# Moving the softmax bias to ScalarE, keeping a sum in PSUM, and rescheduling the end of attention and the output-weight splits

## The chip, the cores and the metric

The kernel runs on one core of a Trainium2 chip. A core has a matrix engine (TensorE, PE in the profile), a vector engine (VectorE, DVE), a scalar engine (ScalarE, ACT), a general-purpose engine (GpSimd, POOL) and an engine that mostly issues DMA transfers (SyncE, SP). Each engine works through its own queue in order and waits on semaphores for the others. The metric is the device time of one execution in microseconds (us), as a median over runs.

## The reference

Two independent computations on inputs with 2048 rows and 1024 columns, whose results stand side by side in the output.

```python
# A: attention with 32 heads of width 32 and a sliding window of 256 keys
q, k, v = split(x @ wqkv)                       # 2048 x 1024 each
scores = (q @ k.T) * 32 ** -0.5                 # per head
scores = where(0 <= i - j < 256, scores, -1e9)
o = softmax(scores) @ v
a = o @ wo
# B: Fourier mixing, real part, by matrix products
ar, ai = xb @ hid_re.T, xb @ hid_im.T
b = seq_re @ ar - seq_im @ ai
out = concat([a, b])
```

All inputs are float32. The kernel splits every float32 operand into a high and a low float16 half (`split`: ScalarE writes the high half, VectorE the difference) and makes each product of three float16 passes.

## The kernel before

The work runs in this order on TensorE. First 96 products for q, k and v, then 64 "units" of Fourier mixing, numbered 0 to 63 in names such as `u61`, `un61_a`, `p2_61_0`, then 8 output products `po`. A unit is of kind x (two products of 24 matmuls) or c (seven products of 12 matmuls, made by `seven`, in which three accumulating PSUM banks `m0`, `m1`, `m2` are drained after each product by ScalarE or VectorE into the `y` tiles). Units 56 to 63 are the last eight of kind c; the code calls their place among the eight `i`, so that `i == 5` is unit 61, `i == 6` unit 62 and `i == 7` unit 63. While a unit runs, the next unit's operands are loaded (`raw_u`), scanned for their largest value on ScalarE (`junk`), reduced through a transposition on TensorE (`pt_u`, `sc_u`) and split (`un62_a`, `un62_b`, `un62_c`); four differences of a unit are made on GpSimd (L621, `gsub`).

Attention runs underneath from product 24 on. It has 256 blocks (128 queries, two heads). `tick` is called every 4 or 8 matmuls and advances the attention generator at a constant `rate`, so that attention ends about 0.7 units before `i == LAST`; there a loop emits what is left, the attention pool `att` is closed and the pool `late` takes its place in SBUF. A block goes through the engines like this:

- TensorE writes scores to one of two PSUM buffers `s` (L210).
- VectorE masks (L218), takes the negative row maximum `mx` (L220) and makes the bias of the exponential, `bias = mx * es + PSHIFT` (L223), two numbers a partition.
- ScalarE takes the exponential, one head at a time, with that bias (L230), and the high half (L233); VectorE makes the low half (L234), which frees the scores' buffer.
- SP transposes both halves by a DMA (L236); GpSimd masks the transposed tile (L248, L250) behind a small instruction `mark` that reads `bias` (L227).
- For each second block TensorE multiplies by v into the only buffer of the pool `ps_v` (tag `pv`, L277). VectorE takes the reciprocal of the row sums (L283), adds the two halves of o into the SBUF tile `os` (L285) and multiplies them by the reciprocal (L288). The transposition `pt_u` of a unit's scale uses the same PSUM buffer.

After attention the output weight `wo` is loaded in eight pieces of 512 KB (`raw_wo0_0` to `raw_wo3_1`), and made into seven operands in two halves: 14 "fills" (a `split` each, into `reg2` and `ext`) and 8 differences on GpSimd. `o_load` and `o_blocks` fetch attention's result and combine it into the operands of the output products (L804, L753, L806, L813).

The order of instructions on each engine is set by a scheduler when the program is built, from the order of the code, the buffers and estimated durations; `tc.issue_after` pins an instruction behind another one.

Of the kernel before, what the change touches and what calls it, by code (L numbers as in the profile page):

```python
# [9 lines left out]
F32 = mybir.dt.float32  # L10
# [40 lines left out]
def fused_kernel(ctx: ExitStack, tc: tile.TileContext, xa, wqk, wv, wo, xb, wd, cs, out):  # L51
# [35 lines left out]

    nbank = [0]
# [50 lines left out]
    def scale_of(key, v, s, down=2.0 ** -14):  # L139

        pt = ps_v.tile([P, 2, 2, VW], F32, tag="pv", name=f"pt_{key}")
        pt = pt.rearrange("p r h w -> p (r h w)")[:, :P]
# [27 lines left out]
    def attention():  # L170
# [22 lines left out]
        def s_step(b, j):  # L193
# [29 lines left out]
            nc.vector.tensor_scalar(bias, mx, es, PSHIFT, op0=ALU.mult, op1=ALU.add)  # L223
# [30 lines left out]
        def v_step(b):  # L254

            g, sc, hp, i = blocks[b]
            pvt = ps_v.tile([P, 2, 2, VW], F32, tag="pv", name=f"pv_{b}")
# [26 lines left out]
            os_ = att.tile([P, 2, 2, DH], F32, tag="os", name=f"os_{b}")  # L284
# [77 lines left out]
    LAST = 6  # L362
# [396 lines left out]
    def wo_blocks(late, i):  # L759

        b1, b2, b3, b4 = (load_raw(wo[b % 2, 2 * (b // 2) + i], [2, CH], f"wo{b}_{i}", late) for b in range(4))

        def fill(pos, raw):
            o = slot(pos)
            split(o[:, 0, 2 * i:2 * i + 2], o[:, 1, 2 * i:2 * i + 2], raw, vwo[:, 1:2])

        def step(turn):
            if turn == 0:
                fill(0, b1)
                gsub(b2, b2, b1)  # L770
            elif turn == 1:
                fill(6, b4)
                gsub(b4, b4, b2)
            elif turn == 2:
                fill(3, b3)
                gsub(b1, b4, b1)
            elif turn == 3:
                fill(4, b2)
                gsub(b3, b3, b4)
            elif turn == 4:  # L780
                fill(2, b4)
            elif turn == 5:
                fill(1, b1)
            elif turn == 6:
                fill(5, b3)

        return step
# [56 lines left out]
    with tc.tile_pool(name="pb", bufs=1) as pb:  # L844
# [62 lines left out]
        for n, (kind, p, c, i) in enumerate(units):  # L907
# [21 lines left out]
            if p == 1 and c == 1:  # L929
                if i == LAST:  # L930
# [7 lines left out]
                    wo_step = wo_blocks(late, 0)  # L938
                if i == LAST + 1:
                    wo_step = wo_blocks(late, 1)  # L940
            late_unit = p == 1 and c == 1 and i >= LAST

            def turned(turn):
                hook(n, turn)
                if late_unit:
                    wo_step(turn)

# [17 lines left out]
            seven(f"p2_{n}", i, uns.pop(n), lambda pos: tsum[:, TPOS[pos]], done, turned)  # L965
            if p == 1 and c == 1 and i == 6:
                o_load(0)
                o_load(1)
                o_blocks(late, 0)
# [63 lines left out]
```

## Time and profile before

| | |
|---|---|
| median of 3 runs | 1881.85 us (1872.96, 1881.85, 1882.64) |
| profiled execution | 1872.75 us |
| its span (first to last instruction) | 1870.9 us |
| TensorE busy | 1776.4 us (95%) |
| VectorE busy | 1349.3 us (72%) |
| ScalarE busy | 984.0 us (53%) |
| GpSimd busy | 670.2 us (36%) |

A row of the groups reads: line, engine, operation, output<-input, shapes, count | busy us, mean ns of one | idle time of the engine ahead of it, and what ended that. In the table of windows the columns are the stretch, its length, busy us and instructions of PE, PEld (weight loads), DVE, ACT and POOL, the mean clock that TensorE was granted (1.00 is full), the share of time the DMA engines were busy and GB/s. The stage names that the prediction uses are: 645 to 1640 us, units with attention underneath; 1640 to 1712 us, the end of the units, where the output weight is prepared; 1712 us to the end, the output products.

### The profile page before, as it was taken

The page shows a single profiled execution, that of the slowest core. Times are in us where ns is not written, and L with a number is a line of the kernel's source. Part 1 is how long each engine was busy: PE and PEld are TensorE (multiplying, and loading weights), DVE is VectorE, ACT ScalarE, POOL GpSimd, SP SyncE. Part 2 cuts the span into 40 slices and gives each one's busy share as a digit, 9 for nine tenths or more (in the row PEclk, how much of TensorE's full clock was granted, in tenths as well). Part 3 has the DMA queues.
Part 4 walks back from the last instruction along what each step waited for, and adds up shares of the span by engine and source line. Part 5 has one row for each costly group of instructions (what it writes and reads, how often), then busy time and mean ns, then how long its engine had stood idle before and what let it go on. Part 6 is the DMA issues. An engine that isn't in the chain of part 4 may idle for free.

```text
span 1870.9 us, 30051 instructions
## 1 busy us (share of the span) xinstructions
PE 1776.4 (95%) x10876; PEld 860.7 (46%) x10876; DVE 1349.3 (72%) x2470; ACT 984.0 (53%) x1567; POOL 670.2 (36%) x849
## 2 busy tenths in 40 slices
PE   7999999999999999999989999988999999879998
PEld 3444555445555544544444444543444445424443
DVE  7665788777666688876787876786787688686551
ACT  3233444454445567755566665675575676543221
POOL 0000122122213554543454543544555456654000
PEclk9999999999999999999999999999999999989999
DMA  5457899886676557777359889557899549865341
GB/s 225 127 180 198 219 240 233 229 217 153 164 166 139 107 127 181 194 184 173 74 123 193 174 178 207 108 125 141 165 175 213 105 105 147 135 163 96 99 120 68
DMA packets 440596, 297.95 MB, mean 159 GB/s; under 512 B 339072, under 2 KB 396416, under 8 KB 440448
## 3 DMA queue, kind: packets, MB, share of 16 engines
q1 hardware_dynamic: 433536, 270.87, 59.9%
q0 software_dynamic: 6912, 25.17, 8.3%
q8 instruction: 85, 1.39, 0.3%
q14 instruction: 63, 0.52, 0.1%
HBM read 146.93 MB, written 75.63 MB: 119 GB/s over the span
## 4 chain that ended last, share of the span: by engine, by line
PE 64%; DVE 12%; DMA 8%; issue 5%; ACT 5%; POOL 5%; SPq 0%; POOLq 0%; ACTq 0%; DVEq 0%
PE p L834 14%; PE p L342 12%; PE pk L342 9%; PE pv L342 8%; PE po L834 8%; PE pq L342 7%; DMA t<-hl 4%; PE s L210 3%; PE pv L277 3%; POOL raw_u L621 2%; DVE reg L104 1%; ACT s L230 1%; DVE mx L220 1%; DMA raw_wd<-in_wd_dram 1%; POOL t L250 1%
## 5 line engine op out<-in xcount | busy, mean ns | idle before, releaser
L230 ACT ACTIVATE s<-s,bias,escs 128x256 f32<-128x256 f32 (+1 forms) x512 | 267.2, 530 | 330.1 <-DVE bias L223 280.6
L342 PE MATMUL p<-reg,un 128*128 128x512 f16 x1536 | 351.4, 383 | 1.9 <-DVE un L104 1.9
L234 DVE TENSOR_TENSOR hl<-s,hl 128x512 f16<-128x512 f32 (+1 forms) x256 | 169.7, 667 | 88.0 <-ACT hl L233 87.4
L342 PEld LDWEIGHTS <-un 128*128 128x128 f16 x1536 | 147.5, 98 | 170.9 <-issue 6.6
L227 POOL TENSOR_SCALAR mark<-bias 128x1 f32<-128x1 f32 x128 | 38.9, 304 | 509.3 <-DVE bias L223 465.2
L834 PE MATMUL p<-reg,un_b 128*128 128x512 f16 x768 | 189.7, 392 | 18.0 <-ACT reg L956 5.7
L834 PE MATMUL p<-reg,un_a 128*128 128x512 f16 x768 | 187.9, 386 | 9.9 <-DVE y L954 7.4
L342 PE MATMUL pq<-reg,wu_q 128*128 128x512 f16 x768 | 177.9, 386 | 7.4 <-ACT reg L109 4.3
L834 PE MATMUL p<-reg,un_c 128*128 128x512 f16 x768 | 180.5, 382 | 3.5 <-ACT y L956 1.9
L342 PE MATMUL pk<-reg,wu_k 128*128 128x512 f16 x768 | 174.7, 381 | 2.3 <-ACT wu_k L109 1.6
L621 POOL TENSOR_TENSOR raw_u<-raw_u,raw_u 128x512 f32<-128x512 f32 x96 | 138.8, 1446 | 95.4 <-DVE un_a L104 91.4
L342 PE MATMUL pv<-reg,reg 128*128 128x512 f16 x768 | 172.7, 379 | 0.0
L220 DVE TENSOR_REDUCE mx<-s 128x2 f32<-128x512 f32 (+1 forms) x256 | 170.1, 668 | 2.8
L248 POOL TENSOR_SCALAR_AFFINE_SELECT z<-t 128x512 f16<-128x512 f16 x224 | 156.2, 718 | 36.4 <-DMA t<-hl 29.8
L250 POOL TENSOR_SCALAR_AFFINE_SELECT t<-t 128x512 f16<-128x512 f16 x224 | 166.2, 765 | 0.1
L233 ACT ACTIVATE hl<-s 128x512 f16<-128x512 f32 (+1 forms) x256 | 147.7, 585 | 9.6 <-DMA t<-hl 5.4
L218 DVE COPY_PREDICATED s<-upper,s 128x256 f32<-128x256 uint32 x224 | 93.7, 422 | 70.8 <-PE s L210 68.6
L210 PE MATMUL s<-qk,qk 96*128 96x128 f16 (+2 forms) x704 | 127.5, 277 | 13.9 <-DVE hl L234 13.7
L834 PEld LDWEIGHTS <-un_b 128*128 128x128 f16 x768 | 74.3, 100 | 105.8 <-issue 26.6
L277 PE MATMUL pv<-vt,t 128*128 128x65 f16 x1984 | 114.9, 186 | 7.7 <-POOL t L250 7.6
L342 PEld LDWEIGHTS <-wu_q 128*128 128x128 f16 x768 | 75.0, 99 | 96.3 <-issue 13.1
L834 PEld LDWEIGHTS <-un_a 128*128 128x128 f16 x768 | 74.2, 99 | 95.9 <-issue 12.9
(166 smaller groups left out, 2827.5 us busy)
## 6 DMA issues: line engine op xcount, KB each, us to landing
raw_u<-in_cs_dram SPq DMA_DIRECT2D x64, 512.0 KB, 4.9
qk<-qs SPq DMA_DIRECT2D x192, 128.0 KB, 3.4
out_dram<-y POOLq DMA_DIRECT2D x36, 512.0 KB, 7.4
raw_u<-in_xb_dram SPq DMA_DIRECT2D x32, 512.0 KB, 5.2
vs<-yv SPq DMA_DIRECT2D x32, 260.0 KB, 2.6
vt<-vs SPq DMA_DIRECT2D x32, 260.0 KB, 3.5
raw_x<-in_xa_dram SPq DMA_DIRECT2D x16, 512.0 KB, 10.2
qs<-yq SPq DMA_DIRECT2D x32, 256.0 KB, 2.5
```

The costliest lines, as they stand in the source:

```text
L210: nc.tensor.matmul(s[:, j, at:at + (k1 - k0) * P], q2s[g, sc][:, h, i * P:i * P + P], k2s[g, k0 // QB][:, h, k0 % QB * P:k0 % QB * P + (k1 ...
L218: nc.vector.copy_predicated(s[:, :, 2 * P:3 * P], upper2, s[:, :, :P] if nb == 3 else never2)
L220: nc.vector.tensor_reduce(mx, sv, axis=AX.X, op=ALU.max, negate=True)
L230: nc.scalar.activation(sv[:, h], sv[:, h], AF.Exp, bias=bias[:, h:h + 1], scale=es)
L233: nc.scalar.activation(hi, sv, AF.Copy)
L234: behind[:] = [nc.vector.tensor_tensor(lo, sv, hi, op=ALU.subtract)]
L248: nc.gpsimd.affine_select(out=z, in_=pk, compare_op=ALU.is_gt, fill=0.0, base=0, pattern=[[0, 4], [-1, P]], channel_multiplier=1)
L250: nc.gpsimd.affine_select(out=pk, in_=pk, compare_op=ALU.is_ge, fill=0.0, base=0, pattern=[[0, 4], [1, P]], channel_multiplier=-1)
L277: nc.tensor.matmul(pvt[:, r, j, lo:], weights(part, j, kb), vts[g, k // QB][:, k % QB, at + lo:at + VW], start=(m == 0), stop=(m == len(se ...
L342: nc.tensor.matmul(ps, lhs(hl, d), rhs(hr, d), start=(m == 0), stop=(m == 3 * n - 1))
L621: nc.gpsimd.tensor_tensor(o, a, b, op=op)
L834: nc.tensor.matmul(ps, lhs[pos](hl, k), rhs(pos)[:, hr, k], start=(m == 0 and fresh), stop=(m == 11), skip_group_check=True)
```

## The change

Four edits.

1. The bias is computed by ScalarE: an ACTIVATE with function Identity, `mx * es + pshift`, where `pshift` is a constant tile of one number a partition, set once by GpSimd.
2. The sum of o's halves no longer goes to an SBUF tile `os` but to free columns of the PSUM bank that holds the product itself.
3. `LAST` goes from 6 to 5: attention's `rate` is set so that it ends a unit earlier, and `late` opens a unit earlier.
4. The 14 fills and 8 differences of the output weight ran one at each of the 7 turns of units 62 and 63; now all eight pieces are loaded at the opening of `late` in unit 61, and the 14 steps are dealt out from turn 2 of unit 61 to turn 1 of unit 63. Each fill is pinned behind the latest drain on ScalarE (`behind_act`). The first two `o_load` and the first `o_blocks` move from the end of unit 62 to turns of units 62 and 63.

```diff
@@ -85,6 +85,9 @@
     nc.gpsimd.memset(never, NEG)
     never2 = never.unsqueeze(2).to_broadcast([P, 2, P])
 
+    pshift = const.tile([P, 1], F32, name="pshift")
+    nc.gpsimd.memset(pshift, PSHIFT)
+
     nbank = [0]
 
     def bank(name):
@@ -138,8 +141,7 @@
 
     def scale_of(key, v, s, down=2.0 ** -14):
 
-        pt = ps_v.tile([P, 2, 2, VW], F32, tag="pv", name=f"pt_{key}")
-        pt = pt.rearrange("p r h w -> p (r h w)")[:, :P]
+        pt = ps_v.tile([P, CH], F32, tag="pv", name=f"pt_{key}")[:, :P]
         spreads[:] = [nc.tensor.transpose(pt, tops.pop(key).to_broadcast([P, P]), ident)]
         vec(nc.vector.tensor_reduce, v, pt, axis=AX.X, op=ALU.max)
         vec(nc.vector.tensor_scalar, v.bitcast(U32), v.bitcast(U32), 0x7F800000, None, op0=ALU.bitwise_and)
@@ -220,7 +222,7 @@
             nc.vector.tensor_reduce(mx, sv, axis=AX.X, op=ALU.max, negate=True)
             bias = att.tile([P, 2], F32, tag="bias", bufs=6, name=f"bias_{b}")
             es = esc[g][:, sc:sc + 1]
-            nc.vector.tensor_scalar(bias, mx, es, PSHIFT, op0=ALU.mult, op1=ALU.add)
+            nc.scalar.activation(bias, mx, AF.Identity, bias=pshift, scale=es)
             if b % 2 == 1:
 
                 mark = att.tile([P, 1], F32, tag="mark", bufs=2, name=f"mark_{b}")
@@ -254,7 +256,8 @@
         def v_step(b):
 
             g, sc, hp, i = blocks[b]
-            pvt = ps_v.tile([P, 2, 2, VW], F32, tag="pv", name=f"pv_{b}")
+            pvb = ps_v.tile([P, CH], F32, tag="pv", name=f"pv_{b}")
+            pvt = pvb[:, :4 * VW].rearrange("p (r h w) -> p r h w", r=2, h=2)
             if (g, sc) not in cur:
                 cur[g, sc] = att.tile([P, QB, P], F32, tag="o", bufs=3, name=f"o_{g}_{sc}")
             for r in (1, 0):
@@ -281,7 +284,7 @@
             o = cur[g, sc]
             rs = att.tile([P, 2, 2], F32, tag="rs", name=f"rs_{b}")
             nc.vector.reciprocal(rs, pvt[:, :, :, 2 * DH])
-            os_ = att.tile([P, 2, 2, DH], F32, tag="os", name=f"os_{b}")
+            os_ = pvb[:, 4 * VW:4 * VW + 4 * DH].rearrange("p (r h d) -> p r h d", r=2, h=2)
             nc.vector.tensor_reduce(os_.rearrange("p r h d -> p (r h) d"),
                                     pvt[:, :, :, :2 * DH].rearrange("p r h (k d) -> p (r h) d k", k=2),
                                     axis=AX.X, op=ALU.add)
@@ -359,7 +362,7 @@
     START = 24
     MM_ATT = 24 * (len(order) - START) + 4 * 8 * 48 + 4 * 8 * 84
 
-    LAST = 6
+    LAST = 5
     rate = 2.0 * (NG * NCH * 2 * QB + 2 * LAG) / (MM_ATT - 84 * (8 - LAST + 0.7))
 
     wraw, wun, vw, xraw, held = {}, {}, {}, {}, {}
@@ -756,35 +759,18 @@
 
         return reg2o[:, pos] if pos < 4 else ext[:, pos - 4]
 
-    def wo_blocks(late, i):
-
-        b1, b2, b3, b4 = (load_raw(wo[b % 2, 2 * (b // 2) + i], [2, CH], f"wo{b}_{i}", late) for b in range(4))
+    def wo_blocks(raw, i):
+
+        b1, b2, b3, b4 = raw
 
         def fill(pos, raw):
             o = slot(pos)
-            split(o[:, 0, 2 * i:2 * i + 2], o[:, 1, 2 * i:2 * i + 2], raw, vwo[:, 1:2])
-
-        def step(turn):
-            if turn == 0:
-                fill(0, b1)
-                gsub(b2, b2, b1)
-            elif turn == 1:
-                fill(6, b4)
-                gsub(b4, b4, b2)
-            elif turn == 2:
-                fill(3, b3)
-                gsub(b1, b4, b1)
-            elif turn == 3:
-                fill(4, b2)
-                gsub(b3, b3, b4)
-            elif turn == 4:
-                fill(2, b4)
-            elif turn == 5:
-                fill(1, b1)
-            elif turn == 6:
-                fill(5, b3)
-
-        return step
+            with tc.issue_after(behind_act[0].ins):
+                split(o[:, 0, 2 * i:2 * i + 2], o[:, 1, 2 * i:2 * i + 2], raw, vwo[:, 1:2])
+
+        return [lambda: (fill(0, b1), gsub(b2, b2, b1)), lambda: (fill(6, b4), gsub(b4, b4, b2)),
+                lambda: (fill(3, b3), gsub(b1, b4, b1)), lambda: (fill(4, b2), gsub(b3, b3, b4)),
+                lambda: fill(2, b4), lambda: fill(1, b1), lambda: fill(5, b3)]
 
     os_, oq = {}, {}
 
@@ -935,16 +921,14 @@
                     att_cm.__exit__(None, None, None)
                     late = ctx.enter_context(tc.tile_pool(name="late", bufs=8, side="right"))
                     ext = late.tile([P, 3, 2, 4, CH], F16, tag="ext", bufs=1, name="ext")
-                    wo_step = wo_blocks(late, 0)
-                if i == LAST + 1:
-                    wo_step = wo_blocks(late, 1)
-            late_unit = p == 1 and c == 1 and i >= LAST
-
-            def turned(turn):
-                hook(n, turn)
-                if late_unit:
-                    wo_step(turn)
-
+                    raw = [[load_raw(wo[b % 2, 2 * (b // 2) + k], [2, CH], f"wo{b}_{k}", late) for b in range(4)]
+                           for k in range(2)]
+                    for k in range(2):
+                        for j, f in enumerate(wo_blocks(raw[k], k)):
+                            do(n + (7 * k + j + 2) // 7, (7 * k + j + 2) % 7, f)
+                    do(n + 1, 3, o_load, 0)
+                    do(n + 1, 5, o_load, 1)
+                    do(n + 2, 2, o_blocks, late, 0)
             y1, y2 = ytile(), ytile()
             f = fu.pop(n)
 
@@ -962,11 +946,8 @@
                     else:
                         nc.gpsimd.dma_start(dst, src, accum_op=ALU.add)
 
-            seven(f"p2_{n}", i, uns.pop(n), lambda pos: tsum[:, TPOS[pos]], done, turned)
-            if p == 1 and c == 1 and i == 6:
-                o_load(0)
-                o_load(1)
-                o_blocks(late, 0)
+            seven(f"p2_{n}", i, uns.pop(n), lambda pos: tsum[:, TPOS[pos]], done,
+                  lambda turn: hook(n, turn))
         copy = lambda y, ps: nc.scalar.activation(y, ps, AF.Copy, scale=fo)
         add = lambda y, ps: nc.vector.scalar_tensor_tensor(y, ps, fo, y, op0=ALU.mult, op1=ALU.add)
         for q in range(NT // 2):
```

The scheduler moves instructions everywhere. Three places follow, in the program's names with their numbers (`s_204` is block 204, `p2_61_3` the product of unit 61 at position 3).

The first place is VectorE and ScalarE at attention blocks 204 and 205. Before, VectorE's queue:

```order
L218 COPY_PREDICATED s_204_14801<-upper_88,s_204_14801 128x2x128
L954 SCALAR_TENSOR_TENSOR reg1_81<-p2_43_3_14973,fu43_14666,reg1_81 128x512
L220 TENSOR_REDUCE mx_204_14832<-s_204_14801 128x2
L223 TENSOR_SCALAR bias_204_14834<-mx_204_14832,escs_109 128x2
L234 TENSOR_TENSOR hl_203_14742<-s_203_14713,hl_203_14742 128x512
L234 TENSOR_TENSOR hl_204_14838<-s_204_14801,hl_204_14838 128x512
L218 COPY_PREDICATED s_205_14862<-upper_88,s_205_14862 128x2x128
L283 RECIPROCAL rs_200_14925<-pv_200_14899 128x4
L285 TENSOR_REDUCE os_200_14927<-pv_200_14899 128x128
L220 TENSOR_REDUCE mx_205_14880<-s_205_14862 128x2
L218 COPY_PREDICATED s_206_14959<-upper_88,s_206_14959 128x2x128
L288 TENSOR_TENSOR o_6_1_14900<-os_200_14927,rs_200_14925 128x2x64
```

Now, ScalarE's queue at the same blocks:

```order
L225 ACTIVATE bias_204_14638<-mx_204_14636,pshift_93,escs_111 128x2
L611 ACTIVATE junk_6356,top_u44_14807<-raw_u44_1_14617 128x1024
L232 ACTIVATE s_204_14604<-s_204_14604,bias_204_14638,escs_111 128x256
L112 ACTIVATE un43_a_14740<-raw_u43_0_14401,sc_u43_14663 128x1024
L112 ACTIVATE reg1_81<-raw_u43_1_14370,sc_u43_14663 128x512
L940 ACTIVATE y2_6359<-p2_42_0_14674,fu42_14399 128x512
L232 ACTIVATE s_204_14604<-s_204_14604,bias_204_14638,escs_111 128x256
L225 ACTIVATE bias_205_14692<-mx_205_14690,pshift_93,escs_111 128x2
L235 ACTIVATE hl_204_14642<-s_204_14604 128x512
L232 ACTIVATE s_205_14655<-s_205_14655,bias_205_14692,escs_111 128x256 x2
```

The 256 bias instructions leave VectorE's queue and stand in ScalarE's, each ahead of its block's exponentials, in 148 of 256 blocks right ahead. Between the sum of o's halves and its product stood on average 1.7 other VectorE instructions (none in 8 of 128 cases), and now 0.6 (none in 67).

The second place is VectorE's queue where the output weight's fills begin. Before (L104 is the fill or split, L954 a drain):

```order
L954 SCALAR_TENSOR_TENSOR y0_6339<-p2_61_1_18670,fu61_18451,y0_6339 128x512
L753 TENSOR_TENSOR r0_1_18896<-r0_1_18896,r0_0_18895 128x512
L104 SCALAR_TENSOR_TENSOR un62_c_18699<-raw_u62_1_18425,sc_u62_18609,un62_c_18699 128x1024
L104 SCALAR_TENSOR_TENSOR reg2_82<-raw_wo0_1_18909,sc_wo_103,reg2_82 128x1024
L753 TENSOR_TENSOR r0_0_18895<-r0_0_18895,r0_1_18896 128x512
L104 SCALAR_TENSOR_TENSOR reg2_82<-raw_wo0_0_18750,sc_wo_103,reg2_82 128x1024
L104 SCALAR_TENSOR_TENSOR reg2_82<-raw_wo2_1_18913,sc_wo_103,reg2_82 128x1024
L954 SCALAR_TENSOR_TENSOR y0_6339<-p2_61_0_18620,fu61_18451,y0_6339 128x512
L104 TENSOR_REDUCE sc_u63_18736<-pt_u63_18737 128x1
L104 SCALAR_TENSOR_TENSOR ext_18749<-raw_wo2_0_18754,sc_wo_103,ext_18749 128x1024
L104 SCALAR_TENSOR_TENSOR un62_b_18733<-raw_u62_0_18453,sc_u62_18609,un62_b_18733 128x1024
```

Now (L107 is the fill or split, L938 a drain):

```order
L938 SCALAR_TENSOR_TENSOR reg1_81<-p2_61_3_18532,fu61_18361,reg1_81 128x512
L107 SCALAR_TENSOR_TENSOR ext_18498<-raw_wo3_0_18505,sc_wo_105,ext_18498 128x1024
L107 SCALAR_TENSOR_TENSOR reg2_82<-raw_wo2_0_18503,sc_wo_105,reg2_82 128x1024
L107 SCALAR_TENSOR_TENSOR ext_18498<-raw_wo1_0_18501,sc_wo_105,ext_18498 128x1024
L107 TENSOR_REDUCE top1_u63_18604<-top_u63_18582 128x1
L790 TENSOR_TENSOR r0_0_18836<-raw_o0_18728 128x1024
L107 SCALAR_TENSOR_TENSOR un62_c_18600<-raw_u62_1_18335,sc_u62_18483,un62_c_18600 128x1024
L938 SCALAR_TENSOR_TENSOR y0_6357<-p2_61_1_18568,fu61_18361,y0_6357 128x512
L107 TENSOR_REDUCE sc_u63_18643<-pt_u63_18644 128x1
L107 SCALAR_TENSOR_TENSOR reg2_82<-raw_wo0_0_18499,sc_wo_105,reg2_82 128x1024
L107 TENSOR_SCALAR sc_u63_18643<-sc_u63_18643 128x1
L938 SCALAR_TENSOR_TENSOR y0_6357<-p2_61_0_18515,fu61_18361,y0_6357 128x512
```

Between the drains of `p2_61_1` and `p2_61_0` stood three fills and now stands one. Counted from the first fill to `un63_b`, the last split that a unit's product waits for, VectorE's queue held 14 fills, 8 splits of `un62` and `un63`, 12 instructions of `o_blocks` and 6 drains; now it holds 11 fills, 6 splits, 9 instructions of `o_blocks` and 4 drains. The other three fills stand behind `un63_b`. On TensorE, the first fill stands at the end of unit 61's product `p2_61_0` in both; from there to the product that reads `un63_b` there were 14 products of 12 matmuls and there are 13.

The third place is SP's queue at the end of attention (`ots_59` in DRAM holds attention's result; `raw_o` reads it back). Before:

```order
L96 DMA raw_u63_0_18618<-in_cs_dram 128x1024
L300 DMA_TRANSPOSE ot_7_3_18518<-ohl_7_3_18515 128x8x128
L301 DMA ots_59<-ot_7_3_18518 128x1024
L96 DMA raw_wo0_0_18750<-in_wo_dram 128x1024
L96 DMA raw_wo1_0_18752<-in_wo_dram 128x1024
L96 DMA raw_wo2_0_18754<-in_wo_dram 128x1024
L96 DMA raw_wo3_0_18756<-in_wo_dram 128x1024
L795 DMA raw_o0_18887<-ots_59 128x16x128
L795 DMA raw_o1_18889<-ots_59 128x16x128
L96 DMA raw_wo0_1_18909<-in_wo_dram 128x1024
L96 DMA raw_wo1_1_18911<-in_wo_dram 128x1024
```

Now:

```order
L304 DMA ots_59<-ot_7_3_18263 128x1024
L99 DMA raw_u63_1_18464<-in_cs_dram 128x1024
L99 DMA raw_wo0_0_18499<-in_wo_dram 128x1024
L99 DMA raw_wo1_0_18501<-in_wo_dram 128x1024
L99 DMA raw_wo2_0_18503<-in_wo_dram 128x1024
L99 DMA raw_wo3_0_18505<-in_wo_dram 128x1024
L99 DMA raw_wo0_1_18507<-in_wo_dram 128x1024
L99 DMA raw_wo1_1_18509<-in_wo_dram 128x1024
L99 DMA raw_wo2_1_18511<-in_wo_dram 128x1024
L99 DMA raw_wo3_1_18513<-in_wo_dram 128x1024
L99 DMA raw_u63_0_18492<-in_cs_dram 128x1024
L781 DMA raw_o0_18728<-ots_59 128x16x128
```

The eight weight loads now stand in one row, ahead of the last unit's second load and of the first loads of attention's result. TensorE's last attention product moved from `p2_60_1` of unit 60 to `p2_59_1` of unit 59.

## The prediction

> **What bounds the kernel now.** I read the page first, then the windows by stage, then who TensorE waited for in each stage. TensorE is busy 95% of the span, so only its gaps, and what they do to its clock, can be won.
>
> ```profile
> span 1870.9 us, 30051 instructions
> PE 1776.4 (95%) x10876; PEld 860.7 (46%) x10876; DVE 1349.3 (72%) x2470; ACT 984.0 (53%) x1567; POOL 670.2 (36%) x849
> 840.00:1140.00 300.00, 275.15 (x1738) 133.33 (x1737) 226.65 (x419) 184.80 (x299) 141.36 (x162) 0.96 0.75 158
> 1140.00:1290.00 150.00, 140.92 (x945) 69.69 (x943) 113.72 (x211) 94.96 (x157) 76.56 (x89) 0.99 0.62 133
> 1290.00:1640.00 350.00, 329.31 (x2150) 162.56 (x2148) 260.45 (x500) 218.08 (x353) 185.83 (x215) 0.97 0.78 149
> 1640.00:1712.00 72.00, 55.23 (x220) 23.02 (x218) 62.38 (x55) 34.22 (x39) 43.74 (x22) 0.86 0.56 131
> 1712.00:1870.00 158.00, 153.79 (x712) 69.46 (x710) 66.90 (x76) 37.41 (x48) 1.73 (x2) 1.00 0.36 100
> ```
>
> The first three windows are attention over the Fourier units: of 800 us TensorE is idle 54.6. Their granted clocks of 0.96, 0.99 and 0.97 take away up to 12 + 1.5 + 10.5 = 24 us more, since a matmul behind a gap runs slower; so an idle microsecond costs 1.4. VectorE is busy 601 of the 800 us (75%), ScalarE 498 (62%). The fourth window, where the output weight is prepared, is worst for its length: 16.8 us idle, clock 0.86, VectorE busy 87%. Behind it almost nothing is lost. These are the waits in 645 to 1640 us and in 1640 to 1712 us:
>
> ```profile
> PE pv L277 <- POOL z L248: 13.5, 5, 6.6
> PE s L210 <- DVE hl L234: 13.1, 11, 2.6
> PE pv L277 <- POOL t L250: 7.7, 11, 2.4
> PE p L834 <- ACT reg L956: 5.9, 5, 2.4
> PE pv L277 <- DVE sc_u L104: 5.8, 2, 2.9
> PE p L834 <- ACT un_b L109: 2.4, 2, 1.8
> PE p L834 <- ACT y L956: 2.2, 4, 1.1
> PE p L342 <- DVE un L104: 1.9, 2, 1.7
> ...
> PE p L834 <- DVE y L954: 10.7, 3, 5.3
> PE p L834 <- DVE un_a L104: 2.5, 1, 2.5
> ```
>
> In the attention stage VectorE ended 20.8 us by these rows, some 25 with smaller ones left out; GpSimd's masks 21.2, ScalarE 10.5. At the end VectorE ended nearly all.
>
> **Bias on ScalarE.** VectorE's price is the first row below, ScalarE's is not in the trace and comes from the exponential's two forms, which also take a bias and a scale by partition.
>
> ```profile
> L223 DVE TENSOR_SCALAR bias<-mx,escs 128x2 f32<-128x2 f32 x256 | 82.5, 327 | 2.2
> L230 ACT ACTIVATE s<-s,bias,escs 128x256 f32<-128x256 f32 x480 | 254.0, 536 | 303.4 <-DVE bias L223 263.8 <-DVE scw L104 10.7 <-DVE sc_u L104 9.6
> L230 ACT ACTIVATE s<-s,bias,escs 128x128 f32<-128x128 f32 x32 | 13.7, 430 | 26.7 <-DVE bias L223 16.8 <-PE pt_u L143 5.4 <-DVE scw L104 4.2
> L223 DVE TENSOR_SCALAR bias<-mx,escs x256: 211/222/1845, 158.7 to 1613.7; 128x2 f32<-128x2 f32 x128
> L288 DVE TENSOR_TENSOR o<-os,rs x128: 276/283/2034, 183.2 to 1631.9; 128x128 f32<-128x128 f32 x128
> L285 DVE TENSOR_REDUCE os<-pv x128: 385/394/415, 182.0 to 1631.5; 128x128 f32<-128x256 f32 x128
> L608 ACT ACTIVATION_READ_ACCUMULATOR junk<-raw_u 128x1 f32 x64 | 12.6, 197 | 0.0
> L288 DVE TENSOR_TENSOR o<-os,rs 128x128 f32<-128x128 f32 x128 | 52.7, 411 | 0.3
> ```
>
> 536 less 430 is 106 ns for 128 columns, so 430 - 106 = 324 ns stay for almost no columns; the shortest ScalarE instruction here, 197 ns, is the lower bound. I take 325: 83 us more on ScalarE, 82.5 less on VectorE. A block's chain hardly changes: 327 ns leave it and 325 enter. What changes is the queue that is shared.
>
> Behind each bias stand its exponentials, the high half and whatever the scheduler put there, drains of product banks among them; those are what TensorE could then wait for. GpSimd's `mark` now waits for ScalarE, and behind it stand the masks; as ScalarE sat idle for the bias through 264 us, it will usually be early.
>
> **Sum kept in PSUM.** The minimum and median of L288 are 276 and 283 ns and its mean is 411, as with the bias (222 and 327): both read only SBUF, and stretch. L285, which reads PSUM, goes from 385 to 415 only. With one operand in PSUM I expect L288 near 283: 128 x 128 ns = 16 us less. If a write into PSUM were slower it would take that back: 0 to 16. The price is that the one `pv` buffer now comes free behind L288 and no longer behind L285.
>
> ```profile
> 1004.94 0.29 PE L143 MATMUL pt_u<-ident,top_u 128*128 128x128 f32 x1 [0.20 <-DVE os L285]
> ...
> 1008.20 0.28 DVE L288 TENSOR_TENSOR o<-os,rs 128x128 f32<-128x128 f32 x1
> ```
>
> Here the next write into that buffer came 3.5 us before L288 had ended, and would have had to wait. In the timeline this holds in 7 of the 128 pairs, by 12.7 us together. That is the upper bound; since the two instructions now stand closer in the queue (0.6 others between them, not 1.7), I take 1.5 us, with the clock 2. Below nothing I see no reason.
>
> **What the attention stage wins.** VectorE loses 82.5 + 16 = 99 us, some 70 of them in these 995 us, so its load of 76% becomes 69%. I let the waits behind a queue go as load over idle share: 0.76/0.24 = 3.2 becomes 0.69/0.31 = 2.2, 30% less. Of 25 us that is 7.7, with the clock **10.8 saved**; bounds 0 (if bursts decide, not the mean) and 25 x 1.4 = 35. ScalarE gains 325 ns for some 170 blocks, 55 us or 5.5%, and goes from 62% to 68%: 1.63 becomes 2.1, 30% more of 10.5, with the clock **4.6 lost**; bounds 0 and 30. GpSimd's 21.2 us I leave: the longest came from a transposition that took 13.76 us on the chain of waits and that no edit touches.
>
> ```profile
> 1294.08 13.76 DMA t<-hl
> ```
>
> **Attention a unit shorter.** The divisor of the rate goes from 5952 - 226.8 to 5952 - 310.8, so attention is 1.5% denser. At a slope of about two, 3% of some 57 us of waits: **1.7 lost**; bounds 0 and 5. Unit 60 has nothing under it then.
>
> **The output weight.** A product lasts 12 of these matmuls, at 137.28/636 = 216 ns: 2.59 us.
>
> ```profile
> 1725.77 137.28 PE po L834 x636
> 1644.69 1.28 DVE L104 SCALAR_TENSOR_TENSOR reg<-raw_wo,sc_wo,reg 128x1024 f16<-128x1024 f32 x1 [3.01 <-ACT reg L109]
> 1665.54 3.37 DVE L104 SCALAR_TENSOR_TENSOR reg<-raw_wo,sc_wo,reg 128x1024 f16<-128x1024 f32 x1
> 1706.57 1.27 DVE L104 SCALAR_TENSOR_TENSOR un_b<-raw_u,sc_u,un_b 128x1024 f16<-128x1024 f32 x1
> L104 DVE SCALAR_TENSOR_TENSOR reg<-raw_wo,sc_wo,reg 128x1024 f16<-128x1024 f32 x8 | 15.3, 1925 | 4.8 <-ACT reg L109 4.8
> L104 DVE SCALAR_TENSOR_TENSOR ext<-raw_wo,sc_wo,ext 128x1024 f16<-128x1024 f32 x6 | 9.6, 1612 | 0.0
> L753 DVE TENSOR_TENSOR r<-r,r 128x512 f32<-128x512 f32 x6 | 8.2, 1373 | 0.0
> L954 DVE SCALAR_TENSOR_TENSOR y<-p,fu,y 128x512 f32<-128x512 f32 x6 | 4.5, 742 | 1.0 <-PE p L834 1.0
> ```
>
> From the first fill (1644.69) to the end of the last unit's split `un_b` (1707.84) VectorE's queue took 63.2 us, idle for some 4 of them (the fills' 4.8 less the 3.01 ahead of the first, the rest for attention's result); in it TensorE had 14 products, 36.3 us. It was 27 us behind there, about the 26 that the window's idle time and clock come to. Now the same stretch has three fills fewer (25 us/14 = 1.78 each: 5.3), three `o_blocks` instructions (4.1), two drains (1.5) and two splits (about 1 us each): 59 - 12.9 = 46 us of work against 13 products, 33.6. It would be 12.4 behind, 14.5 better. Against that stand loads in one row, eight of 512 KB ahead of the last unit's second load and of attention's result; the first instruction that reads this (L790 in the changed kernel) stands ahead of a drain. I give 4.5 of the 14.5 back for such waits: **10 saved**. Bounds: nothing saved, if VectorE waits as long as it is relieved; 20, if GpSimd, whose differences stretch a fill from 1.28 to 3.37 us, falls less on them. What is late next is still VectorE's queue.
>
> **The sum.** -10.8 + 4.6 + 2 + 1.7 - 10 = -12.5 us, against the profiled execution of 1872.75 us (span 1870.9 and 1.85 around it): **1860.3 us**. The three runs shown are 1872.96, 1881.85 and 1882.64, so the profiled execution is level with the lowest and 9 below their median; if the changed kernel spreads alike its median can stand as much above the sum. I forecast 1861. What a measurement of this kernel can tell from no change is 0.5%, 9.4 us about 1881.85.
>
> **The rivals.**
>
> *VectorE's waits go altogether* (0.15). The two longest, for `hl` and `sc_u`, come in bursts where two biases stretched behind GpSimd; without them the queue may not back up at all: 25 x 1.4 = 35 saved, with 15 at the end and 6 lost on ScalarE and the denser attention: 1829 us. Against it: masks, reductions and low halves remain, at 69% load.
>
> *Nothing to speak of* (0.26). The attention stage's gaps come from transpositions stuck behind 512 KB loads, and each reshuffle of the queues only moves them; the end stays bound by VectorE and GpSimd. The terms cancel within 5 us: 1868 to 1878, some 9 higher by the median.
>
> *ScalarE becomes the late queue* (0.15), the other side. A bank's drain that comes more than one product, 2.59 us, late stops TensorE. In the first attention units ScalarE already works 132.34 of 195 us:
>
> ```profile
> 645.00:840.00 195.00, 190.45 (x1270) 94.98 (x1267) 160.58 (x310) 132.34 (x217) 95.25 (x112) 0.99 0.68 167
> ```
>
> That is 68%, and 73% with the bias. It decides once bias and exponentials stand ahead of two drains in a burst: if the 10.5 us of waits for ScalarE grow fourfold, 31 x 1.4 = 44 are lost, and with 11 saved on VectorE, 10 at the end and 4 lost elsewhere the time is 1900 us. For it: the bias is pinned in front of exponentials that wait for VectorE, so ScalarE can now also stand idle in a bias. Against it: it stood idle in the exponential at that point before.
>
> The Trainium skill, page "ScalarE: Activation LUTs", section "Rules for kernel authors", has adds and multiplies on VectorE and not on ScalarE, which speaks for this rival; its section "What ACT_TABLE_LOAD costs" puts an ACTIVATE at 186 ns + 0.833 ns an element and some 93 ns for each operand by partition, an estimate of 374 ns for this bias, 96 us in all, and by it the loss on ScalarE in the sum would be 5.3 instead of 4.6. No row of this trace shows such an instruction yet.
>
> **Chances.** The forecast, 1845 to 1870, 0.44; the other three as given. My own range for the forecast alone is 1845 to 1872; for 8 in 10 it takes in most of the first two rivals: 1835 to 1886. Faster by over 0.5% is under 1872.4: nearly all of the forecast, the first rival and a little of the second, 0.62. Within 0.5%: 0.23. Slower: 0.15.
>
> **What would show it.** L288 near 285 ns and the bias on ScalarE near 325; VectorE's busy time near 1250 us, ScalarE's near 1067. TensorE's waits for `hl` and `sc_u` down from 19 to some 12 us, for ScalarE's drains up by 3. In the last units: 13 products with VectorE some 46 us from the first fill to the last `un_b`, and no wait there over 4 us. The forecast is wrong if waits for ScalarE in the attention stage pass 25 us, if a wait for `pv` behind L288 appears often, or if VectorE stands still at the end for attention's result.

## The result, and the profile after

The changed kernel takes 1850.26 us (median of 4 runs, 1849.88 to 1854.13) against 1882.24 us (median of 4, 1872.96 to 1882.90): a ratio of 0.9846, 95% interval 0.9813 to 0.9879. It is 1.5% faster. The forecast was 1861 us, its range 1835 to 1886. The profiled execution took 1849.88 us, 22.9 less than that of before.

From the page of the changed kernel, the span and the busy times:

```profile
span 1848.2 us, 30067 instructions
PE 1764.0 (95%) x10876; PEld 857.3 (46%) x10876; DVE 1300.3 (70%) x2214; ACT 1064.5 (58%) x1823; POOL 668.4 (36%) x850
```

The groups by shape (busy us, mean ns of one, idle time ahead and its end) show the bias and the product that were changed, the sum, and one untouched instruction:

```profile
L225 ACT ACTIVATE bias<-mx,pshift,escs 128x2 f32<-128x2 f32 x256 | 98.3, 384 | 252.3 <-DVE mx L222 234.9 <-DVE rs L286 12.8 <-DVE s L220 2.4
L291 DVE TENSOR_TENSOR o<-pv,rs 128x128 f32<-128x128 f32 x128 | 36.5, 285 | 2.3
L288 DVE TENSOR_REDUCE pv<-pv 128x128 f32<-128x256 f32 x128 | 54.2, 424 | 1.0
L672 DVE TENSOR_TENSOR reg<-y,reg 128x1024 f16<-128x1024 f32 x32 | 45.9, 1439 | 9.3 <-ACT reg L671 9.2
```

The last row is one that no edit touched; it reads and writes only SBUF, and stood at 1341 ns before. By itself it shows nothing of the change: in the other order of the changed kernel (e7 below) it stands at 1341 again, and with the bias on VectorE it runs from 1292 to 1388 by the order.

```profile
L669 DVE TENSOR_TENSOR reg<-y,reg 128x1024 f16<-128x1024 f32 x32 | 42.9, 1341 | 17.7 <-ACT reg L668 17.7
```

TensorE's waits from 640 to 1720 us, before and then after (what waits, for whom: us in total, times, longest). `hl` fell from 13.1 to 5.9 us, GpSimd's masks `z` and `t` fell from 21.2 to 14.2, and ScalarE's drains did not rise:

```profile
PE pv L277 <- POOL z L248: 13.5, 5, 6.6
PE s L210 <- DVE hl L234: 13.1, 11, 2.6
PE p L834 <- DVE y L954: 12.5, 6, 5.3
PE pv L277 <- POOL t L250: 7.7, 11, 2.4
```

```profile
PE p L820 <- DVE y L938: 12.1, 5, 5.8
PE pv L280 <- POOL z L250: 8.5, 4, 3.4
PE s L212 <- DVE hl L236: 5.9, 5, 3.0
PE p L820 <- DVE un_b L107: 5.9, 3, 4.1
PE p L820 <- ACT y L940: 5.9, 8, 1.7
PE pv L280 <- POOL t L252: 5.7, 6, 1.5
PE pt_u L145 <- DVE o L291: 5.0, 2, 4.8
PE pv L280 <- DVE sc_u L107: 2.8, 2, 2.6
```

The changed kernel runs ahead, so the same microseconds don't hold the same work. I therefore count what TensorE lost in each piece of work: the time from the end of one matmul to the end of the next, less 216 ns for 512 columns (the prediction's row of `po`), narrower ones in proportion, summed between the first matmuls of two units. Gaps and slower matmuls are both in it.

| lost us in | before | after |
|---|---|---|
| products for q, k, v (attention underneath from the 24th) | 17.7 | 13.6 |
| units of kind x (four groups of eight) | 20.1 | 10.0 |
| units of kind c: 8 to 15 | 3.3 | 8.6 |
| 24 to 31 | 30.4 | 30.8 |
| 40 to 47 | 23.2 | 14.1 |
| 56 to 59 | 12.9 | 8.5 |
| 60 to 63 | 25.2 | 24.1 |
| output products | 5.4 | 5.4 |

23 us are gained, 17.9 of them in the units with attention, 4 in the products before them, and 1 where the output weight is prepared. The forecast had 2.5 in the first and 10 in the last. The time was near the forecast; the gain was about twice the sum's 12.5 us, and its seat was another.

### The profile page after: what moved, and what is told of

Its sections match the earlier page's. It is cut to its first block, busy times and chain, and to the rows that moved or that the text cites. A ratio compares the mean times of both kernels' runs of the same rounds, so it can differ in the third digit from the quotient of the medians.

```text
span 1848.2 us, 30067 instructions
## 1 busy us (share of the span) xinstructions
PE 1764.0 (95%) x10876; PEld 857.3 (46%) x10876; DVE 1300.3 (70%) x2214; ACT 1064.5 (58%) x1823; POOL 668.4 (36%) x850
## 4 chain that ended last, share of the span: by engine, by line
PE 65%; DVE 10%; DMA 7%; ACT 7%; issue 6%; POOL 5%; SPq 0%; POOLq 0%; ACTq 0%; DVEq 0%
PE p L820 15%; PE p L345 12%; PE pk L345 9%; PE po L820 8%; PE pq L345 8%; PE pv L345 8%; PE s L212 3%; DMA raw_wd<-in_wd_dram 3%; DMA t<-hl 3%; PE pv L280 3%; POOL raw_u L624 2%; DVE un_c L107 2%; DVE reg L107 1%; ACT s L232 1%; DVE mx L222 1%
## 5 line engine op out<-in xcount | busy, mean ns | idle before, releaser
L225 ACT ACTIVATE bias<-mx,pshift,escs 128x2 f32<-128x2 f32 x256 | 98.3, 384 | 252.3 <-DVE mx L222 234.9
L229 POOL TENSOR_SCALAR mark<-bias 128x1 f32<-128x1 f32 x128 | 48.6, 380 | 457.5 <-ACT bias L225 449.0
L820 PE MATMUL p<-reg,un_b 128*128 128x512 f16 x768 | 191.1, 392 | 19.6 <-DVE un_b L107 5.9
L250 POOL TENSOR_SCALAR_AFFINE_SELECT z<-t 128x512 f16<-128x512 f16 x224 | 152.4, 704 | 25.9 <-DMA t<-hl 25.2
L820 PEld LDWEIGHTS <-un_b 128*128 128x128 f16 x768 | 74.4, 100 | 110.4 <-issue 24.7
L820 PEld LDWEIGHTS <-un_a 128*128 128x128 f16 x768 | 75.3, 99 | 96.7 <-issue 13.1
```

The source lines that it names most:

```text
L225: nc.scalar.activation(bias, mx, AF.Identity, bias=pshift, scale=es)
L250: nc.gpsimd.affine_select(out=z, in_=pk, compare_op=ALU.is_gt, fill=0.0, base=0, pattern=[[0, 4], [-1, P]], channel_multiplier=1)
L820: nc.tensor.matmul(ps, lhs[pos](hl, k), rhs(pos)[:, hr, k], start=(m == 0 and fresh), stop=(m == 11), skip_group_check=True)
```

## The experiments

**The same work in another order.** `acc` is the accumulator that paces attention. Another start shifts attention against the units by a fraction of a step and changes no instruction. (A step is 5725/528 = 10.8 matmuls, so half a step is five or six, not the two that the first expectation says.)

```diff
-    acc = [0.0]
+    acc = [0.5]      # 0.25 and 0.75 in two others
```

> The kernel before with one number changed: the accumulator that paces attention starts at 0.5 instead of 0, so every step of attention falls half a step (some 2 of TensorE's matmuls) earlier, and not one instruction more or less is issued. Theory 'load' (attention's gain comes from VectorE's shorter queue): the time stays within 3 us of the kernel before, and the idle time of TensorE stays about 145 us. Rival 'reshuffle' (each new order of the queues lets the bursts fall elsewhere, and the gain is such a draw): it moves by 5 us or more either way, with VectorE's busy time unchanged at 1349 us.

> The kernel before with attention's accumulator started at 0.25. Theory 'reshuffle, and nothing else' (e1, e5 and e7 moved by 7 to 11 us where no cost changed or a cost rose; so the kernel before was one of the slow orders): of this run and e10 at least one lies at 1862 us or below, and their mean is under 1868. Rival 'the three edits are worth some 25 us in every order': both lie at 1866 to 1882 us.

> The kernel before with attention's accumulator started at 0.75. As for the start at 0.25: 'reshuffle, and nothing else': one of the two at 1862 us or below; 'worth some 25 us in every order': both at 1866 to 1882 us.

> The changed kernel with attention's accumulator started at 0.5 instead of 0, and no instruction more or less. The kernel before moved by -0.4% with this (e1). Theory 'VectorE's queue is short enough now': the time moves by under 4 us, 1846 to 1854 us. Rival 'reshuffle': it moves by 8 us or more, to 1842 or below or to 1858 or above.

Measured: the kernel before goes to 1866.71 us at 0.25 (ratio 0.9936, 0.9897 to 0.9975), 1868.03 at 0.5 (0.9961, 0.9926 to 0.9995), 1881.82 at 0.75 (1.0005, 0.9986 to 1.0025); the changed kernel at 0.5 to 1838.85 (0.9790, 0.9737 to 0.9843). So an order alone moves the kernel before by up to 12 us (the intervals at 0.25 and 0.75 do not meet), as 'reshuffle' says; but none of its four orders reaches 1862 us, and there the other theory held. The changed kernel moves by 11 us, though its two intervals meet.

**One edit alone.** The first edit alone, at start 0 and at 0.5; the second alone; the last two alone.

```diff
-            nc.vector.tensor_scalar(bias, mx, es, PSHIFT, op0=ALU.mult, op1=ALU.add)
+            nc.scalar.activation(bias, mx, AF.Identity, bias=pshift, scale=es)
```

> The kernel before with the first edit alone: the bias is made on ScalarE. Theory 'load': VectorE's busy time 68 us lower, about 1281 (before, 68.2 of the bias's 83.7 us did not overlap a neighbour), less what other instructions stretch; attention gains 9 to 12 us of the 13.8 that the whole change gained before unit 60's end; time 10 us below the kernel before. Rival 'reshuffle': the time can fall anywhere from 10 us less to 5 us more. Rival 'ScalarE late': slower, with waits for ScalarE's drains over 25 us.

> The kernel before with the first edit alone (e2) and attention's accumulator started at 0.5 (e1). Theory 'the bias is worth something in every order': below e1's 1868 us by 10 us or more. Theory 'reshuffle, and nothing else': anywhere from 1840 to 1880 us, with even chances of more and less than 1860.

```diff
-            os_ = att.tile([P, 2, 2, DH], F32, tag="os", name=f"os_{b}")
+            os_ = pvb[:, 4 * VW:4 * VW + 4 * DH].rearrange("p (r h d) -> p r h d", r=2, h=2)
```

> The kernel before with the second edit alone: the sum of o's halves stays in the PSUM bank. Theory 'load': the product of o falls from 411 to 285 ns, the sum rises from 395 to 424, VectorE's busy time 5 us lower (10.7 less 6 us, by the parts that overlap no neighbour); time 0 to 2 us less. Rival 'bank held': waits for pv or pt_u behind the product of o of some 5 us, time 2 to 5 us more. Rival 'reshuffle': 5 us or more either way with none of these waits.

```diff
-    LAST = 6
+    LAST = 5
...
+                    for k in range(2):
+                        for j, f in enumerate(wo_blocks(raw[k], k)):
+                            do(n + (7 * k + j + 2) // 7, (7 * k + j + 2) % 7, f)
```

> The kernel before with the third and fourth edits alone: attention a unit shorter and the output weight's splits dealt out. My sum: 10 less at the end and 1.7 more in attention, 8 us below the kernel before; the loss of TensorE over units 60 to 63, 33 us before, 23 to 25. If the end's gain needed the relieved VectorE of the other edits: under 4 us gained.

Measured: the bias alone 1848.75 us (0.9840, 0.9804 to 0.9876), three times what 'load' gave it; but at start 0.5 it is 1877.95 (0.9990, 0.9971 to 1.0010), no faster than the same start with the bias on VectorE (10 us slower by the medians, 5 by the ratios, whose intervals meet). So 'worth something in every order' failed. The sum in PSUM alone 1878.10 (1.0002, 0.9976 to 1.0028), as 'load' had it, with the product of o at 285 ns. The end alone 1872.91 (0.9962, 0.9935 to 0.9990), 6 to 7 us of the 8 expected; its units 60 to 63 lost 23.1 us. (The 33 us that the expectation gives for before counted from inside unit 59; from unit 60 on they are 25.2, so 2 were gained there. The execution that was profiled took 1875.54 us, no less than that of before, so its trace does not show where the other 4 to 5 us of the median lie.)

In the groups of the kernel with the first edit alone the product of o, still in SBUF, stands at 438 ns (411 before). Here too one row shows little: with `os` in SBUF it runs from 377 to 454 ns in the five kernels with the bias on VectorE, and from 436 to 469 in the three without.

```profile
L291 DVE TENSOR_TENSOR o<-os,rs 128x128 f32<-128x128 f32 x128 | 56.0, 438 | 1.0
```

**One edit undone.** The changed kernel with the bias on VectorE again, at start 0 and 0.5, and with `os` in SBUF again.

```diff
-            nc.scalar.activation(bias, mx, AF.Identity, bias=pshift, scale=es)
+            nc.vector.tensor_scalar(bias, mx, es, PSHIFT, op0=ALU.mult, op1=ALU.add)
```

> The changed kernel with the first edit undone: the bias is made on VectorE again, the rest stays. Theory 'bias alone carries it': 1869 to 1878 us, ratio to the kernel before 0.995 to 1.0. Theory 'the edits add' (my sum's form): the two other edits keep their 8 us at the end, and with the bias worth 28 us alone the time is some 1870 us; the two theories part only in e6 and in the changed kernel itself. Rival 'reshuffle': under 1860 us, since a draw could have favoured this order too.

> The changed kernel with the first edit undone (e5) and attention's accumulator started at 0.5 (e7). If e5's 1843 us was a lucky order and the bias is worth 10 us or more: 1850 to 1868 us, above e7's 1839. If the bias on ScalarE is worth nothing here: within 5 us of e7, and by 'reshuffle, and nothing else' anywhere from 1835 to 1880 us.

```diff
-            os_ = pvb[:, 4 * VW:4 * VW + 4 * DH].rearrange("p (r h d) -> p r h d", r=2, h=2)
+            os_ = att.tile([P, 2, 2, DH], F32, tag="os", name=f"os_{b}")
```

> The changed kernel with the second edit undone: os goes to SBUF again. Theory 'bias alone carries it': within 3 us of the changed kernel, 1847 to 1853 us. Rival 'bank held' (the product of o holds pv longer, and costs the 5 us wait for pt_u): 1842 to 1847 us, and no wait for pt_u behind VectorE over 1 us. Theory 'the edits add', with e3's 0: 1850 us.

Measured: without the bias on ScalarE 1843.49 us (0.9831, 0.9782 to 0.9881), as fast as the changed kernel; at start 0.5, 1864.45 (0.9934, 0.9896 to 0.9973), 26 slower than the changed kernel there. Without the sum in PSUM 1858.30 (0.9900, 0.9868 to 0.9933), 8 us more and outside all three expectations, though the intervals just meet. 'Bias alone carries it', which I had formed on the run of the bias alone, fell with the first of these, and so did 'the edits add' (1870); 'reshuffle' had it under 1860. The run at start 0.5 came as it should if the first was a lucky order and the bias is worth 10 us or more (1850 to 1868).

**VectorE loaded again.** The bias is made on both engines; VectorE's goes into a tile that nobody reads.

```diff
             nc.scalar.activation(bias, mx, AF.Identity, bias=pshift, scale=es)
+            bias2 = att.tile([P, 2], F32, tag="bias2", bufs=6, name=f"bias2_{b}")
+            nc.vector.tensor_scalar(bias2, mx, es, PSHIFT, op0=ALU.mult, op1=ALU.add)
```

> The changed kernel and, beside the bias on ScalarE, the old bias instruction on VectorE as well, right behind the row maximum, into a tile that nobody reads. The way from the row maximum to the exponential stays the short one. Theory 'load on VectorE': VectorE's busy time some 60 us up to 1360, time back up by 15 to 28 us, 1865 to 1878 us. Rival 'chain' (the gain is the step from VectorE to ScalarE taken out between maximum and exponential): under 5 us lost, 1848 to 1855 us.

Measured: 1843.91 us (0.9831, 0.9782 to 0.9880), not slower than the changed kernel. The busy times of its page, and then three rows of TensorE's waits from 640 to 1720 us:

```profile
PE 1764.0 (96%) x10876; PEld 857.6 (47%) x10876; DVE 1331.8 (72%) x2470; ACT 1068.4 (58%) x1823; POOL 662.9 (36%) x850
```

```profile
PE s L212 <- DVE hl L238: 10.7, 7, 3.6
PE pv L282 <- POOL z L252: 7.0, 4, 4.4
PE pv L282 <- POOL t L254: 6.0, 7, 1.5
```

VectorE has all its 2470 instructions back, and the wait for `hl` is back too, 10.7 us; the time is not, so 'load on VectorE' failed here. 'Chain' is not shown either: the changed kernel with the bias on VectorE has the long chain and the same time (1843.49). The masks waited for are 13.0 us here.

**The fourteen orders together.** The first five columns say which kernel it is; then the median, and of the profiled execution the span, TensorE's waits from 640 to 1720 us, and what ended them (sums over the rows of the view of waits).

| run | bias on | sum in | end | start | median us | span | waits | VectorE (of it `hl`) | ScalarE | GpSimd |
|---|---|---|---|---|---|---|---|---|---|---|
| before | V | SBUF | old | 0 | 1882 | 1870.9 | 75.3 | 39.8 (13.1) | 14.3 | 21.2 |
| e9 | V | SBUF | old | 0.25 | 1867 | 1856.0 | 66.7 | 31.4 (10.7) | 19.6 | 15.7 |
| e1 | V | SBUF | old | 0.5 | 1868 | 1864.2 | 67.2 | 25.5 (9.1) | 21.3 | 20.4 |
| e10 | V | SBUF | old | 0.75 | 1882 | 1879.2 | 82.9 | 34.5 (8.8) | 19.3 | 29.1 |
| e3 | V | PSUM | old | 0 | 1878 | 1871.7 | 80.7 | 43.1 (13.7) | 24.4 | 13.2 |
| e4 | V | SBUF | new | 0 | 1873 | 1873.8 | 85.0 | 38.2 (8.2) | 24.7 | 22.1 |
| e2 | S | SBUF | old | 0 | 1849 | 1848.7 | 69.5 | 32.4 (7.2) | 17.3 | 19.8 |
| e11 | S | SBUF | old | 0.5 | 1878 | 1870.4 | 81.8 | 20.2 (2.9) | 25.7 | 35.9 |
| e5 | V | PSUM | new | 0 | 1843 | 1839.7 | 62.6 | 39.0 (7.2) | 15.7 | 7.9 |
| e12 | V | PSUM | new | 0.5 | 1864 | 1867.6 | 75.3 | 43.2 (17.8) | 12.9 | 18.6 |
| e6 | S | SBUF | new | 0 | 1858 | 1855.6 | 69.2 | 34.4 (9.4) | 5.8 | 29.0 |
| after | S | PSUM | new | 0 | 1850 | 1848.2 | 66.4 | 37.8 (5.9) | 12.3 | 14.2 |
| e7 | S | PSUM | new | 0.5 | 1839 | 1843.3 | 58.3 | 33.3 (3.4) | 13.5 | 11.5 |
| e8 | S and V | PSUM | new | 0 | 1844 | 1842.2 | 61.8 | 32.6 (10.7) | 16.2 | 13.0 |

The start alone moves the two kernels that have only some of the edits further than the four of before: by 28 us with the bias alone (e2 and e11), and by 19 us with the sum and the end (e5 and e12).

Three readings. First, span and waits go together (correlation 0.92), 1.42 us of span for each us waited (standard error 0.18): near the prediction's 1.4. Second, the waits that VectorE ended don't follow the span (0.05); those of ScalarE (0.50) and GpSimd (0.63) do, loosely, as far as fourteen points can tell. GpSimd's run from 7.9 to 35.9 us while its busy time stays within 660 to 681. What it waits for itself is the transposition of `hl` (over the fourteen its idle time for that and TensorE's waits for GpSimd have a correlation of 0.70): in two kernels that differ in the start alone (bias on ScalarE, start 0, then 0.5), the group of the first mask reads

```profile
L251 POOL TENSOR_SCALAR_AFFINE_SELECT z<-t 128x512 f16<-128x512 f16 x224 | 155.9, 717 | 43.6 <-DMA t<-hl 43.5
```

```profile
L251 POOL TENSOR_SCALAR_AFFINE_SELECT z<-t 128x512 f16<-128x512 f16 x224 | 166.1, 760 | 77.8 <-DMA t<-hl 73.1
```

Third, all three edits together against none: three orders with a mean ratio of 0.9822 (after, e7, and e8 with its extra instruction) against four with 0.9976 (before, e9, e1, e10), 29 us apart at 1879 us, and no order of one set reaches the other. The spread inside a set is 5 to 6 us (standard deviation), so the 29 are good to some 4, or to some 7 by the wider spread of the fit below. What each edit is worth is not settled by this. A fit of one figure per edit to the fourteen ratios gives the bias 12.9 us (standard error 4.2), the sum in PSUM 7.5 (5.5) and the end 9.3 (6.7), and leaves 9.8 us per order unexplained; it rests on the edits adding up, and the runs of one edit and of two speak against taking that closely (at start 0 the last two edits gain 1.7% together, and nothing and 0.4% apart).

The lowest median is that of the changed kernel with the start at 0.5, 1838.85 us; its interval meets those of the changed kernel, e2, e5 and e8.

## Why the prediction was right, and where it was not

**What bounds the kernel: held.** TensorE's work is the same 10876 matmuls; its idle time fell by 10.3 us (94.5 to 84.2) and its busy time by 12.4, with the mean granted clock up from 0.977 to 0.986 (busy time times clock agrees within 0.3%). Over the fourteen kernels 1.42 us of span went with each us waited; in this pair 22.7 us went with 10.3 us of idle time, 2.2 each.

**Bias on ScalarE, the price: too low.** 325 ns was read out of two forms of the exponential, 384 were measured. By the Trainium skill, page "ScalarE: Activation LUTs", section "What ACT_TABLE_LOAD costs", it was 374 (an estimate): nearer.

**VectorE's relief: half the size, for a reason that the sum left out.** It fell by 49 us and not by 99. The page's busy time counts overlapping instructions once: of the biases' durations only 68.2 us lay behind the end of the instruction before, and of the product's drop only 10.7. And the sum in PSUM costs 29 ns more each, 6.2 us by that count, and some 24 us came back elsewhere: 15 of them are in instructions that no edit touched and that last longer here, 1318.6 us in all against 1303.9 (the others I did not trace). Over the fourteen kernels this is smaller but there: 1310 us in the mean of the five with the bias on ScalarE alone, 1301 in the nine others. That it is GpSimd's instructions that now stretch these in place of the bias is likely, but not shown. The Trainium skill, page "SBUF — State Buffer", section "Who interferes with whom", says that a VectorE instruction with two SBUF inputs contends with a GpSimd instruction that reads SBUF, and that issue order decides who blocks; by that rule it ends for the product of o, which now has one input in PSUM: the trace agrees, 411 to 285 ns.

**The attention stage's gain: right in direction, the term mis-sized.** 10.8 less 4.6, 2 and 1.7 made 2.5; 17.9 were measured in the units with attention. Waits for `hl` and `sc_u` were to fall from 19 to 12 and fell to 8.7 (5.9 and 2.8). That part is more than one draw: `hl` is 11.0 us in the mean of the nine kernels with VectorE's instruction and 5.8 in the five without, at 1.42 a gain of 7 if no other wait takes its place. The largest other fall in this order is that of the masks, 21.2 to 14.2 us, which I had left alone as touched by no edit; the fourteen orders show that they fall and rise with the order. Load over idle share as a rule for a wait is thus not shown: with VectorE's load put back, `hl` came back, and the time did not, though one order cannot show 7 us against a spread of 10.

**ScalarE's loss of 4.6, and its rival as late queue (0.15): not seen.** Its load rose as forecast (1064.5 us, expected 1067), yet the waits it ended are 12.3 us, and 14.9 in the mean of the five kernels with the bias on ScalarE alone against 18.7 in the other nine. The rule of the Trainium skill, page "ScalarE: Activation LUTs", section "Rules for kernel authors", puts adds and multiplies on VectorE and not on ScalarE. The traces agree on the price of one instruction (327 ns in the mean on VectorE, 384 on ScalarE); that the kernel gets slower by breaking it they don't bear out.

**The bank held longer, 1.5 us, with the clock 2: of the right size.** `pt_u` waited 5.0 us behind the product of o, 4.8 of them at once. But there VectorE spent 4.35 us in `un_c` beside GpSimd, with the reciprocal, the sum and the product all behind it; the product adds 0.33 us to the end of the sum:

```profile
1579.64 4.35 DVE L107 SCALAR_TENSOR_TENSOR un_c<-raw_u,sc_u,un_c 128x1024 f16<-128x1024 f32 x1 [4.44 <-ACT un_c L112]
1583.91 0.17 DVE L286 RECIPROCAL rs<-pv 128x4 f32<-128x4 f32 x1
1584.11 0.43 DVE L288 TENSOR_REDUCE pv<-pv 128x128 f32<-128x256 f32 x1
1584.58 0.29 DVE L291 TENSOR_TENSOR o<-pv,rs 128x128 f32<-128x128 f32 x1
```

With `os` in SBUF and the bias alone the same wait stands at 4.4 us behind the sum. In the other order of the changed kernel (e7) it is 9.7 us in five. Counted as the time from the end of the sum to the end of the product, and no more than the wait, the edit's part is 0.5 us here, 2.6 in e7, and under 1 in the four other kernels with the sum in PSUM.

**The output weight, 10 saved: the step that failed.** VectorE's queue from the first fill to `un63_b` was 48 us (forecast 46), but units 60 to 63 gained 1.1 us here, and 2.7 in the mean of seven kernels each way (25.9 to 23.2; single kernels scatter from some 19 to 30). The 13 products that I set against the queue were read from the order of instructions; the trace has 135 matmuls in it, 11 products or 29 us, so that TensorE was some 19 us behind there by the same sum, and not 12.4. These windows (us, then busy us of PE, PEld, DVE, ACT and POOL, granted clock, DMA share, GB/s) and lines of the timeline show what stood in the way:

```profile
1600.00:1632.00 32.00, 30.01 (x141) 13.61 (x140) 12.24 (x18) 14.93 (x20) 17.56 (x14) 1.00 0.91 256
1632.00:1680.00 48.00, 33.81 (x135) 13.95 (x133) 47.35 (x36) 23.25 (x27) 27.89 (x14) 0.87 0.35 61
```

```profile
1607.58 2.34 POOL L624 TENSOR_TENSOR raw_wo<-raw_wo,raw_wo 128x1024 f32<-128x1024 f32 x1 [4.66 <-DMA raw_wo<-in_wo_dram]
1629.38 0.69 ACT L940 ACTIVATE y<-p,fu 128x512 f32<-128x512 f32 x1 [1.90 <-PE p L820]
1631.00 1.14 ACT L112 ACTIVATE ext<-raw_wo,sc_wo 128x1024 f16<-128x1024 f32 x1
```

```profile
1616.60 0.75 DVE L938 SCALAR_TENSOR_TENSOR y<-p,fu,y 128x512 f32<-128x512 f32 x1 [9.75 <-PE p L820]
1632.17 1.98 DVE L107 SCALAR_TENSOR_TENSOR ext<-raw_wo,sc_wo,ext 128x1024 f16<-128x1024 f32 x1 [3.63 <-ACT ext L112]
1669.54 2.92 DVE L107 SCALAR_TENSOR_TENSOR reg<-raw_wo,sc_wo,reg 128x1024 f16<-128x1024 f32 x1
1672.38 2.83 DVE L756 TENSOR_TENSOR r<-r,r 128x512 f32<-128x512 f32 x1
1675.13 3.37 DVE L107 SCALAR_TENSOR_TENSOR ext<-raw_wo,sc_wo,ext 128x1024 f16<-128x1024 f32 x1
1679.03 1.27 DVE L107 SCALAR_TENSOR_TENSOR un_b<-raw_u,sc_u,un_b 128x1024 f16<-128x1024 f32 x1
```

```profile
1669.66 5.22 PE L820 MATMUL p<-reg,un_b 128*128 128x512 f16 x12 [5.85 <-DVE y L938]
1680.35 4.02 PE L820 MATMUL p<-reg,un_b 128*128 128x512 f16 x9 [4.10 <-DVE un_b L107]
```

GpSimd's first difference of the weight ran at 1607.6 us, so the first pieces were there, and the piece that the first fill in the queue reads (`raw_wo3_0`) had landed by 1612.4. But that fill is dealt to turn 3 of unit 61 and pinned behind the drain of the product at position 1, which ScalarE made at 1629.4; so its high half came at 1631.0 and its low half at 1632.2. In between VectorE stood idle, once for 9.75 us. Then it was busy for 47.35 of 48 us, and three of its last instructions, beside GpSimd, were stretched to 2.83 to 3.37 us. TensorE stood still for two waits of 5.85 and 4.10 us, so "no wait over 4 us there" was wrong. Earlier fills, without that pin, might use the idle stretch; that was not tried, so that the late start cost the gain is argued, not shown.

**What it did not reckon with.** The rival 'nothing to speak of' had it that a reshuffle of the queues only moves the gaps. Its time (1868 to 1878 us) did not come, but its mechanism did, in e11 and e12 above all. Its premise, transpositions late behind 512 KB loads, is in the traces: before, the transpositions of `hl` that SP issued while such a load from an input was in flight landed after 4.7 us in the median, 15 of 143 after more than 8 us; of the 113 others the median is 3.1 us, and one took more than 8. In e11 22 of 140 took more than 8 us behind a load, in e5 7 of 122. The sum takes one order of the queues as given. The same work in another order differs by some 10 us, and in e2 and e11 by 28, more than the 12.5 us of the sum. So it was partly luck that the forecast of 1861 and its range held: the two largest terms were wrong in opposite directions, the attention stage's too small and the output weight's too large.

## What to carry to other kernels

Here the bounding engine is 95% busy and its gaps are some 60 waits of about a microsecond, and two orders of the same instructions differed by as much as a good edit. In such a kernel run each version in three or four shifted orders before you credit an edit, and keep the fastest order. A wait that disappears is only worth its row if no other takes its place, so compare the sum of the waits, not the one that was aimed at. And an order of instructions tells what stands behind what, not when: the first fill, pinned behind a drain, came 19 us after its data.

## What was unexpected of the hardware

GpSimd stood idle for late transpositions ahead of the same 224 masks for 43.5 or 73.1 us by the order alone, and for 22.7 to 73.1 us over the fourteen kernels. A sum of VectorE written into PSUM and not SBUF took 424 ns in place of 395. The time by which the bias and the product were stretched (222 ns the median of the bias, 327 its mean) did not all leave with them: of 43 us, 256 x 105 ns and 128 x 128 ns (411 less 283), some 15 came back in untouched instructions in this order, and some 9 in the mean of the orders.
